# Attention and two feed-forward layers on one core: value products three units behind the scores, paired column blocks in the first layer, and an output normalised in halves

## The chip, the cores and the metric

The kernel runs on one core of a Trainium2 chip. The metric is device time in microseconds (us), the median of several runs. A profiled execution gives the trace; its engines are PE (TensorE matmul, with PEld for its weight loads), DVE (VectorE), ACT (ScalarE), POOL (GpSimd) and SP, which here issues all DMAs, transposes among them, from one queue in order. The wide matrix products use pairs of fp16 numbers, a high and a low part, so that each product of two matrices is three matmuls: high by high, high by low, low by high.

## The reference

Clustered attention with 2 batches, 8 heads, 768 positions and head size 64: queries and keys are assigned to the nearest of 16 centroids, and scores between different clusters are masked. Its output, as 1536 tokens of 512 features, goes through two feed-forward layers.

```python
q_assign = np.argmax(np.einsum('bhsd,hcd->bhsc', q_n, c_n), axis=-1)
k_assign = np.argmax(np.einsum('bhsd,hcd->bhsc', k_n, c_n), axis=-1)
mask = q_assign[:, :, :, None] == k_assign[:, :, None, :]
scores = np.where(mask, scale * np.matmul(q, k.transpose(0, 1, 3, 2)), -1000000000.0)
attn = np.exp(scores - np.max(scores, axis=-1, keepdims=True))
attn = attn / (np.sum(attn, axis=-1, keepdims=True) + 1e-09)
x = np.matmul(attn, v)                        # then (1536, 512)
...
h = x @ w_in                                  # layer 1: 512 -> 2048 -> 512
x = (h * (1.0 / (1.0 + np.exp(-h)))) @ w_out
...
h = x @ w2_in                                 # layer 2: 512 -> 2048 -> 512
out = (np.maximum(h, 0.0) + alpha * np.minimum(h, 0.0)) @ w2_out
```

## The kernel before

**Attention.** A unit is one head of one tile of 128 queries: 12 tiles by 8 heads are 96 units, u = 0 to 95. `front(u)` makes the scores (4 matmuls, L458 and L462, into one of two `s` buffers of PSUM), takes their maximum (DVE, L474), the exponential (ACT, L480), its fp16 high part (ACT, L487) and low part (DVE, L489). `front_t(u)` transposes both parts by a DMA (L495) into one of three `pt` buffers. `back(u)` makes the value product from them (18 matmuls, L507, into the one `x` tile). In the program text `back(u - LAG)` stands behind `front(u)`, with `LAG = 2`. After the eighth head of a tile `x_done` multiplies by the inverse sums (L533), makes a high and a low part (L536, L537) and transposes them (L538) as input of layer 1.

**Layer 1** (`layer1`) takes the 12 tiles in seven chunks: two of one tile, five of two. For each of 16 column blocks it makes 12 matmuls into a PSUM tile (L834), then tanh (ACT, L840), a DVE operation that also reads the PSUM tile (L841), the high part (ACT, L844) and the low part (DVE, L845). Then 16 steps of 12 matmuls make the output (L865). A step of L834 is called an A step here, A0 to A111 over the whole kernel, and a step of L865 a B step, B0 to B111.

**Weights.** They arrive as 64-bit numbers in eight pieces per matrix. A piece is loaded (SP, L561), put together as fp32 (ACT L572; ACT L576 or POOL L580; DVE L583 and L586), its squares are summed (ACT L612, and a small matmul with a matrix of ones, L211), and it is scaled and split (POOL L593, L605, L607, L609; DVE L594). The two matrices of layer 2 are loaded over the attention's keys and queries, so their loads wait for the last scores. The scale of the first layer-2 matrix is per piece; that of the second needs the sums of all its eight pieces.

**Layer 2** runs three times over 512 tokens: `split_x2` makes high and low parts of its input (DVE L924), L937 the 16 column blocks (12 matmuls each, called C), with DVE L946, L947 and L951 and ACT L950 between, and L968 the output (called D).

**What sets the order.** Program order is a hand-written interleaving: `UNITS_BY_CHUNK`, `W_TASKS` and `W2_TASKS` say how many units and weight pieces go with each step of layer 1. The framework then orders the instructions of each engine with a timeline of its own, so the order on an engine is not that of the text; it is fixed when the kernel is built, and each engine works through its own list. `issue_after(later, earlier)` adds an order between two instructions to that.

## Time and profile before

| | |
|---|---|
| runs | 878.33 us median of 3 (874.54 to 878.88) |
| profiled execution | 873.64 us; its span from first to last instruction 871.5 us |
| mean granted clock of TensorE | 0.931 of full speed |
| busy share of the span | PE 81%, PEld 56%, DVE 70%, ACT 54%, POOL 18% |
| PE idle before value products (L507), for a transpose | 78.9 us in 48 waits |

The busy shares are means over stages that differ: attention with layer-1 weights, attention with layer 1, conversion of the layer-2 weights, and layer 2. PE's bars are modelled, so a busy PE is not PE at its peak.

### The profile page before, as it was taken

What the parts mean: (1) busy time and instruction counts of PE and PEld (TensorE: products, weight loads), DVE (VectorE), ACT (ScalarE), POOL (GpSimd) and SP (SyncE); (2) the same over time, 40 slices, a digit from 0 to 9 for tenths busy, and PEclk for the clock granted to TensorE, in tenths of its full rate; (3) what the DMA queues carried; (4) which work ended last, traced back from release to release, by engine and by line L of the source; (5) the groups of instructions that cost most, each with busy time, mean ns of one, the idle gap of its engine ahead of it and who ended that gap; (6) DMA issues with size and microseconds to landing.
All of it is one profiled execution on the core that took longest, in us unless ns stands there. A gap on an engine that the chain in (4) does not pass through costs nothing.

```text
span 871.5 us, 16209 instructions
## 1 busy us (share of the span) xinstructions
PE 704.7 (81%) x6484; PEld 487.1 (56%) x6484; DVE 607.4 (70%) x1302; ACT 468.5 (54%) x861; POOL 153.5 (18%) x117
## 2 busy tenths in 40 slices
PE   2435267777887997899898869789969999999998
PEld 1323146675766776788677758667424444444443
DVE  6999988888967777875986777786993058206700
ACT  7837576647857664755765577868541023002200
POOL 5734520340201220000000004341190000000000
PEclk9995567689999999999999999999999999999999
DMA  9999878659896786784778687353100000000000
GB/s 278 235 229 249 252 177 134 122 118 163 143 173 115 119 166 98 138 140 73 123 123 139 118 222 177 116 201 139 48 1 13 24 13 1 13 25 12 1 25 25
DMA packets 241595, 101.86 MB, mean 117 GB/s; under 512 B 217328, under 2 KB 227568, under 8 KB 241392
## 3 DMA queue, kind: packets, MB, share of 16 engines
q1 hardware_dynamic: 241520, 100.83, 54.0%
q8 instruction: 51, 0.84, 0.4%
q14 instruction: 24, 0.20, 0.1%
HBM read 44.08 MB, written 3.15 MB: 54 GB/s over the span
## 4 chain that ended last, share of the span: by engine, by line
PE 36%; DMA 12%; DVE 10%; ACT 4%; issue 2%; POOL 1%; SPq 0%; POOLq 0%; DVEq 0%; ACTq 0%
PE w L968 10%; DMA arena<-arena 8%; PE w L937 6%; PE m L968 5%; PE m L937 4%; PE w L865 3%; PE w L834 3%; DMA arena<-in_moe_w_out_dram 2%; PE x L507 2%; DMA arena<-in_moe_w_in_dram 2%; DVE arena L583 1%; DVE arena L586 1%; PE s L458 1%; PE s L462 1%; DVE arena L951 1%
## 5 line engine op out<-in xcount | busy, mean ns | idle before, releaser
L834 PEld LDWEIGHTS <-arena 128*128 128x128 f16 x1344 | 126.6, 107 | 35.1 <-issue 18.8
L834 PE MATMUL w<-arena 128*128 128x256 f16 (+1 forms) x1212 | 137.5, 273 | 10.6 <-DVE arena L841 8.5
L507 PE MATMUL x<-arena 128*128 128x64 f16 x1728 | 75.0, 202 | 79.9 <-DMA arena<-arena 78.9
L865 PEld LDWEIGHTS <-arena 128*128 128x128 f16 x1344 | 118.5, 100 | 20.7 <-POOL arena L605 2.9
L865 PE MATMUL w<-arena 128*128 128x256 f16 (+1 forms) x1200 | 123.9, 260 | 5.4 <-POOL arena L605 2.5
L507 PEld LDWEIGHTS <-arena 128*128 128x128 f16 x1728 | 66.2, 104 | 95.4 <-DMA arena<-arena 91.8
L489 DVE TENSOR_TENSOR arena<-arena 128x768 f16<-128x768 f32 x96 | 95.0, 991 | 32.3 <-ACT arena L487 32.0
L474 DVE TENSOR_REDUCE stat<-s 128x1 f32<-128x768 f32 x96 | 91.1, 951 | 28.4 <-PE s L462 28.2
L480 ACT ACTIVATE arena<-s,stat 128x768 f32<-128x768 f32 x96 | 94.5, 985 | 26.3 <-DVE stat L478 25.5
L487 ACT ACTIVATE arena<-arena 128x768 f16<-128x768 f32 x96 | 80.5, 842 | 42.0 <-DMA arena<-arena 41.0
L937 PEld LDWEIGHTS <-arena 128*128 128x128 f16 x576 | 57.0, 99 | 80.0 <-issue 15.5
L968 PEld LDWEIGHTS <-arena 128*128 128x128 f16 x576 | 56.4, 98 | 68.0
L580 POOL TENSOR_SCALAR arena<-arena 128x1024 f32<-128x1024 f32 x28 | 43.2, 1541 | 287.2 <-DMA arena<-in_moe_w_in_dram 219.1
L937 PE MATMUL w<-arena 128*128 128x512 f16 x384 | 87.7, 383 | 5.3 <-DVE arena L947 5.3
L458 PE MATMUL s<-arena 80*128 80x384 f16 x192 | 69.8, 364 | 17.6 <-DMA arena<-arena 11.1
L968 PE MATMUL w<-arena 128*128 128x512 f16 x384 | 83.9, 379 | 0.0
L950 ACT ACTIVATE arena<-arena,stat 128x512 f16<-128x512 f32 x48 | 34.5, 720 | 88.2 <-DVE arena L947 86.2
L462 PE MATMUL s<-arena 128*128 128x384 f16 x192 | 69.8, 364 | 0.0
L840 ACT ACTIVATE arena<-w,stat 128x256 f32<-128x256 f32 (+1 forms) x101 | 43.5, 434 | 29.3 <-PE w L834 24.2
L583 DVE SCALAR_TENSOR_TENSOR arena<-arena 128x1024 int32<-128x1024 int32 x32 | 42.9, 1340 | 22.1 <-ACT arena L572 8.3
L946 DVE TENSOR_SCALAR arena<-w,stat 128x512 f32<-128x512 f32 x32 | 24.0, 749 | 46.9 <-PE w L937 46.5
L845 DVE SCALAR_TENSOR_TENSOR arena<-arena 128x256 f16<-128x256 f32 (+1 forms) x112 | 49.7, 451 | 6.0 <-ACT arena L844 5.9
(137 smaller groups left out, 1014.1 us busy)
## 6 DMA issues: line engine op xcount, KB each, us to landing
arena<-in_moe_w_in_dram SPq DMA_DIRECT2D x16, 1024.0 KB, 5.9
arena<-in_moe_w_out_dram SPq DMA_DIRECT2D x16, 1024.0 KB, 5.1
arena<-in_k_dram SPq DMA_DIRECT2D x8, 384.0 KB, 3.8
arena<-in_q_dram SPq DMA_DIRECT2D x6, 512.0 KB, 4.9
arena<-in_v_dram SPq DMA_DIRECT2D x8, 384.0 KB, 5.8
out_dram<-arena SPq DMA_DIRECT2D x12, 256.0 KB, 2.0
arena<-arena SPq DMA_TRANSPOSE x149, 3.9
arena<-in_moe_alpha_dram SPq DMA_DIRECT2D x1, 1024.0 KB, 4.7
```

Of the source, the lines that this page charges most:

```text
L458: nc.tensor.matmul(out=sc[:, j, :hs], lhsT=qt2[0:D + C, h], rhs=kt2[0:D + C, h % 2, j * hs:(j + 1) * hs], start=True, stop=False,)
L462: nc.tensor.matmul(out=sc[:, j, :hs], lhsT=qt1[:, h], rhs=kt1[:, h % 2, j * hs:(j + 1) * hs], start=False, stop=True,)
L474: nc.vector.tensor_reduce(out=nm, in_=sc[:, :, :hs], axis=AX.XY, op=ALU.max, negate=True)
L480: nc.scalar.activation(out=view(o, F32, 2, hs), in_=sc[:, :, :hs], func=ACTF.Exp, scale=scl, bias=bias, accum_out=sums[n % 2][:, h:h + 1],)
L487: nc.scalar.activation(out=hl[:, 0], in_=p, func=ACTF.Copy)
L489: en.tensor_tensor(out=hl[:, 1], in0=p, in1=hl[:, 0], op=ALU.subtract)
L507: nc.tensor.matmul(out=x_ps[0][:, h], lhsT=pt[:, ph * T + t], rhs=vt[:, h % 2, t, vh], start=(i == 0), stop=(i == 3 * T - 1),)
L583: nc.vector.scalar_tensor_tensor(out=lo, in0=hi, scalar=3, in1=lo, op0=ALU.logical_shift_left, op1=ALU.bitwise_or)
L834: nc.tensor.matmul(out=hp, lhsT=wi[:, a, kd, f % 2 * 128:f % 2 * 128 + 128], rhs=mov(bb, kd), start=(i == 0), stop=(i == 3 * KD - 1),)
L865: nc.tensor.matmul(out=acc, lhsT=wo[:, a, f % 2, dt * 128:(dt + 1) * 128], rhs=g[:, f, bb], start=(i == 0), stop=(i == 3 * KF - 1),)
L937: nc.tensor.matmul(out=hp, lhsT=in_piece(o_a + 24 * KB, f // 2)[:, a, kd, f % 2 * 128:][:, :128], rhs=x[bb][:, kd], start=(i == 0), stop=( ...
L968: nc.tensor.matmul(out=acc, lhsT=g[:, f, a, t * 128:(t + 1) * 128], rhs=out_piece(o_w, f // 2)[:, bb, f % 2], start=(i == 0), stop=(i == 3 ...
```

## The change

The value product of unit u is held behind the scores of unit u + 3: `LAG` is 3, and `issue_after` ties the first of its matmuls to the last score matmul of u + 3. `layer1` works on two column blocks at a time: 24 matmuls go into the two halves of one PSUM tile, and tanh, the two DVE operations and the high part each run once over both. `x_done` does its three DVE operations once for each half of the heads, over one smaller buffer `xf`. The buffer of layer 1's intermediate grows from 3 pieces of 1 KB to 2 of 2 KB, and the last targets of `UNITS_BY_CHUNK` are 99, the number of units plus the new lag. The rest of the program text is unchanged.

```diff
-UNITS_BY_CHUNK = (32, 53, 64, 69, 98, 98, 98)
+UNITS_BY_CHUNK = (32, 53, 64, 69, 99, 99, 99)
...
-            nc.tensor.matmul(
+            s_last[u] = nc.tensor.matmul(
                 out=sc[:, j, :hs], lhsT=qt1[:, h],
...
-                nc.tensor.matmul(
+                mm = nc.tensor.matmul(
                     out=x_ps[0][:, h], lhsT=pt[:, ph * T + t], rhs=vt[:, h % 2, t, vh],
                     start=(i == 0), stop=(i == 3 * T - 1),
                 )
+                if i == 0 and u + LAG in s_last:
+                    issue_after(mm, s_last[u + LAG])
...
-        nc.vector.tensor_tensor(out=xf, in0=x_ps[0], in1=bc(rs, D), op=ALU.mult)
...
+        for w in range(2):
+            xf = view(o_xf, F32, 4, D)
+            nc.vector.tensor_tensor(
+                out=xf, in0=x_ps[0][:, 4 * w:4 * w + 4], in1=bc(rs[:, 4 * w:4 * w + 4], D),
+                op=ALU.mult,
+            )
+            xf = view(o_xf, F32, DM // 2)
+            nc.vector.tensor_copy(out=xhl[:, 0, w], in_=xf)
+            nc.vector.tensor_tensor(out=xhl[:, 1, w], in0=xf, in1=xhl[:, 0, w], op=ALU.subtract)
...
-    LAG = 2
+    LAG = 3
...
-        for f in range(KF):
-            j = f // 2
+        for j in range(NPC):
...
-            hp = psum("l", n)
...
+            hp = psum("l", 2, n)
+            for r in range(2):
+                i = 0
+                for kd in range(KD):
+                    for a, bb in ((0, 0), (0, 1), (1, 0)):
+                        nc.tensor.matmul(
+                            out=hp[:, r], lhsT=wi[:, a, kd, r * 128:r * 128 + 128], rhs=mov(bb, kd),
+                            start=(i == 0), stop=(i == 3 * KD - 1),
+                        )
+                        i += 1
+                if r == 0:
+                    yield
+            th = view(o_tmp + 2 * KB * ring("t1", 2), F32, 2, n)
+            nc.scalar.activation(out=th, in_=hp, func=ACTF.Tanh, scale=dh[:, j:j + 1])
             nc.vector.scalar_tensor_tensor(
                 out=th, in0=th, scalar=1.0, in1=hp, op0=ALU.add, op1=ALU.mult
             )
...
+            hi, lo = g[:, 2 * j:2 * j + 2, 0], g[:, 2 * j:2 * j + 2, 1]
+            nc.scalar.activation(out=hi, in_=th, func=ACTF.Copy, scale=2.0 ** -16)
             nc.vector.scalar_tensor_tensor(
...
+                out=lo, in0=th, scalar=2.0 ** -16, in1=hi, op0=ALU.mult, op1=ALU.subtract,
             )
             yield
```

Since the framework orders each engine anew, instructions move far from the edited lines too. Three places matter below. The first is on PE, around the scores of the last unit, u = 95. Before, they stand between two A steps:

```order
L834 MATMUL w<-arena 128x256
L458 LDWEIGHTS arena
L458 MATMUL s<-arena 128x384
L462 LDWEIGHTS arena
L462 MATMUL s<-arena 128x384
...
L834 LDWEIGHTS arena
L834 MATMUL m<-arena 128x256
```

In the change they stand in the middle of chunk 5's B steps (L874 is the old L865, L459 and L463 the old L458 and L462):

```order
L874 MATMUL w<-arena 128x256
L459 LDWEIGHTS arena
L459 MATMUL s<-arena 128x384
L463 LDWEIGHTS arena
L463 MATMUL s<-arena 128x384
...
L874 LDWEIGHTS arena
L874 MATMUL w<-arena 128x256
```

Counted over the whole lists, 92 A steps, 80 B steps and 92 value products stand ahead of these scores before, and 96 A steps, 88 and a quarter B steps and 91 value products in the change.

The second place is also on PE, at the small sums of the second layer-2 matrix (L211 into `s`; L211 into `m` are those of `split_x2`). Before, the last seven of them stand in three places among the last B steps and the first C steps (L937); here are the second three and the last:

```order
L937 MATMUL w<-arena 128x512
L211 MATMUL s<-stat,arena 128x1 x3
L937 LDWEIGHTS arena
...
L937 MATMUL w<-arena 128x512
L211 MATMUL s<-stat,arena 128x1
L937 LDWEIGHTS arena
```

In the change all seven stand together, and the sums of `split_x2` behind them, ahead of the first C step (L946 is the old L937):

```order
L874 MATMUL w<-arena 128x256
L211 MATMUL s<-stat,arena 128x1 x7
L211 MATMUL m<-stat,arena 128x1 x4
L946 LDWEIGHTS arena
L946 MATMUL m<-arena 128x512
```

Eight C steps stood ahead of the last sum before, and none does in the change.

The third place is on DVE, from the scale of the second layer-2 matrix on (L160 from `s`). Before, DVE has the first pass of layer 2 under way there, and the two low parts that it makes for the weights (L594) stand among its rows:

```order
L160 TENSOR_SCALAR stat<-s 128x1
L951 SCALAR_TENSOR_TENSOR arena<-arena,stat 128x512
L947 SCALAR_TENSOR_TENSOR arena<-w,arena 128x512
...
L594 SCALAR_TENSOR_TENSOR arena<-arena,stat 128x1024
L946 TENSOR_SCALAR arena<-w,stat 128x512
L947 SCALAR_TENSOR_TENSOR arena<-w,arena 128x512
L594 SCALAR_TENSOR_TENSOR arena<-arena,stat 128x1024
```

In the change both low parts (L601) come first, then the split of the first pass's input (L933, the old L924), and only then its first row (L955, the old L946):

```order
L593 SCALAR_TENSOR_TENSOR arena<-arena 128x1024
L160 TENSOR_SCALAR stat<-s 128x1
...
L689 TENSOR_SCALAR stat<-stat 128x8
L601 SCALAR_TENSOR_TENSOR arena<-arena,stat 128x1024 x2
L160 TENSOR_SCALAR stat<-m 128x1
...
L933 SCALAR_TENSOR_TENSOR arena<-arena,stat 128x512 x4
L955 TENSOR_SCALAR arena<-m,stat 128x512
```

POOL's list is the same at this place in both: one piece for the first of these low parts, two multiplications of other pieces, and then the piece for the second.

## Rows read from the trace of the kernel before

**Rows 1.** Busy time by stage: start:end, PE, PEld, DVE, ACT, POOL, clock, DMA
```profile
0.00:135.00 135.00, 57.73 (x568) 43.26 (x569) 122.30 (x273) 93.77 (x154) 60.51 (x61) 0.76 0.94 235
135.00:293.00 158.00, 121.83 (x1772) 103.02 (x1770) 128.08 (x322) 105.36 (x224) 30.27 (x19) 0.90 0.80 138
293.00:509.00 216.00, 191.55 (x2246) 157.09 (x2247) 160.82 (x407) 134.55 (x263) 7.33 (x6) 0.98 0.70 122
509.00:603.00 94.00, 78.88 (x732) 67.94 (x730) 72.66 (x128) 72.78 (x135) 29.40 (x18) 0.96 0.60 180
603.00:660.00 57.00, 47.05 (x211) 21.33 (x209) 51.13 (x66) 26.88 (x39) 26.03 (x14) 0.94 0.09 32
660.00:872.00 212.00, 207.66 (x967) 94.42 (x965) 72.37 (x111) 35.12 (x50) 0.00 (x0) 1.00 0.04 15
```

**Rows 2.** Waits of PE from 135 to 293 us: us, times, longest
```profile
PE x L507 <- DMA arena<-arena: 25.7, 19, 2.6
```

**Rows 3.** Waits of PE from 293 to 509 us
```profile
PE x L507 <- DMA arena<-arena: 15.4, 16, 2.2
```

**Rows 4.** Timeline of PE, value products that waited: first and last, of 35
```profile
141.03 0.70 PE L507 MATMUL x<-arena 128*128 128x64 f16 x18 [2.14 <-DMA arena<-arena]
...
505.88 0.70 PE L507 MATMUL x<-arena 128*128 128x64 f16 x18 [1.29 <-DMA arena<-arena]
```

**Rows 5.** Chain that ended last: start us, us, what
```profile
391.80 7.86 PE w L865 x72
...
611.80 4.92 DMA arena<-in_moe_w_out_dram
...
630.13 3.13 POOL arena L607 x2
...
637.07 1.52 DVE arena L951
...
655.31 4.34 PE m L937 x12
659.65 10.36 PE w L968 x48
...
701.09 2.59 PE m L937 x12
```

**Rows 6.** Timeline of PE, 508 to 626 us: start us, us, what
```profile
508.38 0.33 PE L458 MATMUL s<-arena 80*128 80x384 f16 x1
...
559.67 2.72 PE L834 MATMUL m<-arena 128*128 128x256 f16 x12 [2.13 <-DVE arena L841]
...
602.67 5.34 PE L937 MATMUL w<-arena 128*128 128x512 f16 x24
...
625.00 0.28 PE L211 MATMUL s<-stat,arena 128*128 128x1 f32 x2
```

**Rows 7.** Groups by line, shapes apart: count, busy us, mean ns, idle before
```profile
L841 DVE SCALAR_TENSOR_TENSOR arena<-arena,w 128x256 f32<-128x256 f32 x69 | 28.5, 414 | 5.0 <-ACT arena L840 5.0
L845 DVE SCALAR_TENSOR_TENSOR arena<-arena 128x256 f16<-128x256 f32 x80 | 39.3, 495 | 5.7 <-ACT arena L844 5.7
L947 DVE SCALAR_TENSOR_TENSOR arena<-w,arena 128x512 f32<-128x512 f32 x32 | 22.0, 687 | 0.3
L583 DVE SCALAR_TENSOR_TENSOR arena<-arena 128x1024 int32<-128x1024 int32 x32 | 42.9, 1340 | 22.1 <-ACT arena L572 8.3 <-ACT arena L576 6.8 <-POOL arena L580 4.7
L533 DVE TENSOR_TENSOR arena<-x,stat 128x512 f32<-128x512 f32 x12 | 8.2, 683 | 2.6 <-PE x L507 2.6
L536 DVE CAST arena<-arena 128x512 f16<-128x512 f32 x12 | 5.0, 420 | 0.1
L537 DVE TENSOR_TENSOR arena<-arena 128x512 f16<-128x512 f32 x12 | 9.7, 806 | 0.1
```

**Rows 8.** Timeline of DVE: one kind of operation, alone and beside POOL
```profile
612.39 0.75 DVE L951 SCALAR_TENSOR_TENSOR arena<-arena,stat 128x512 f16<-128x512 f32 x1
...
643.06 2.69 DVE L951 SCALAR_TENSOR_TENSOR arena<-arena,stat 128x512 f16<-128x512 f32 x1
```

More of the change, by code (lines that the diff above doesn't have):

```diff
@@ L117, in cluster_attention_silu_prelu @@
     o_xt = region(12 * KB)
-    o_tmp = region(3 * KB)
+    o_tmp = region(4 * KB)
     o_a = region(0)
@@ L129, in cluster_attention_silu_prelu @@
     o_pt = region(NPT * 3 * KB)
-    o_xf = region(2 * KB)
+    o_xf = region(KB)
     o_xhl = region(2 * KB)
@@ L251, in prep_centroids2 @@
         sq = view(o_xf + 256, F32, D)
-        cc = view(o_xf + 512, F16, 3, 128)
+        cc = view(o_xhl, F16, 3, 128)
         ss, y, r = scr(1), scr(1), scr(1)
@@ L445, in cluster_attention_silu_prelu @@
     pt_of = {}
+    s_last = {}
     x_ps = {}
@@ L524, in x_done @@
         assert c < 3 or c - 3 in g1_done
-        xf = view(o_xf, F32, H, D)
         rs = scr(H)
@@ L532, in x_done @@
         )
-        nc.vector.tensor_tensor(out=xf, in0=x_ps[0], in1=bc(rs, D), op=ALU.mult)
-        xf = view(o_xf, F32, DM)
-        xhl = view(o_xhl, F16, 2, DM)
-        nc.vector.tensor_copy(out=xhl[:, 0], in_=xf)
-        nc.vector.tensor_tensor(out=xhl[:, 1], in0=xf, in1=xhl[:, 0], op=ALU.subtract)
+        xhl = view(o_xhl, F16, 2, 2, DM // 2)
+        for w in range(2):
[7 more added lines that the diff above has]
+            nc.vector.tensor_tensor(out=xhl[:, 1, w], in0=xf, in1=xhl[:, 0, w], op=ALU.subtract)
         nc.sync.dma_start_transpose(
             out=view(o_xt + 4 * KB * (c % 3) + 2 * KB * i, F16, 2 * KD, 128),
-            in_=xhl.rearrange("p a b -> p (a b)"),
+            in_=view(o_xhl, F16, 2 * DM),
         )
@@ L821, in layer1 @@
             nc.vector.tensor_scalar(dh, w1["in"].inv, x_inv[b], 0.5, op0=ALU.mult, op1=ALU.mult)
-        for f in range(KF):
-            j = f // 2
+        for j in range(NPC):
             wi = in_piece(o_w, j)
-            if c == 0 and f % 2 == 0:
+            if c == 0:
                 nc.vector.tensor_scalar(
@@ L829, in layer1 @@
                 )
-            hp = psum("l", n)
-            i = 0
-            for kd in range(KD):
-                for a, bb in ((0, 0), (0, 1), (1, 0)):
-                    nc.tensor.matmul(
-                        out=hp, lhsT=wi[:, a, kd, f % 2 * 128:f % 2 * 128 + 128], rhs=mov(bb, kd),
-                        start=(i == 0), stop=(i == 3 * KD - 1),
-                    )
-                    i += 1
-            th = view(o_tmp + KB * ring("t1", 3), F32, n)
-            nc.scalar.activation(out=th, in_=hp, func=ACTF.Tanh, scale=dh[:, f // 2:f // 2 + 1])
+            hp = psum("l", 2, n)
[12 more added lines that the diff above has]
+            nc.scalar.activation(out=th, in_=hp, func=ACTF.Tanh, scale=dh[:, j:j + 1])
             nc.vector.scalar_tensor_tensor(
@@ L843, in layer1 @@
             )
-            nc.scalar.activation(out=g[:, f, 0], in_=th, func=ACTF.Copy, scale=2.0 ** -16)
+            hi, lo = g[:, 2 * j:2 * j + 2, 0], g[:, 2 * j:2 * j + 2, 1]
+            nc.scalar.activation(out=hi, in_=th, func=ACTF.Copy, scale=2.0 ** -16)
             nc.vector.scalar_tensor_tensor(
-                out=g[:, f, 1], in0=th, scalar=2.0 ** -16, in1=g[:, f, 0],
-                op0=ALU.mult, op1=ALU.subtract,
+                out=lo, in0=th, scalar=2.0 ** -16, in1=hi, op0=ALU.mult, op1=ALU.subtract,
             )
```

## The prediction, made before the kernel ran

> **What bounds the kernel now.** I read the busy time by stage first [rows 1]. Up to 135 us DVE is busy for 122.3 of 135 us: layer-1 weights and the first 16 units load it, and nothing that only helps PE pays there. From 135 to 509 us PE has 313 us of work in 374, DVE 289: neither is full, but PE is nearer. From 509 to 603 us PE, DVE and ACT are each at 77 to 84%; this stage converts the layer-2 weights while PE finishes layer 1. From 603 to 660 us DVE is busy 51 of 57 us. From 660 us on PE does layer 2 almost without a gap, 212 us that the change does not touch.
>
> Next the waits of PE. Before value products it waited for transposes for 25.7 us and 15.4 us in the two middle stages [rows 2, 3], 41.1 us of the 61 us that PE was idle there. Such waits before 135 us lie under DVE.
>
> Last, the chain that ended last [rows 5]. Its tail is no attention: a load of the second layer-2 matrix at 611.80, POOL's multiplications at 630.13, DVE at 637.07, then the last C step at 655.31 and the first D step at 659.65. The loads it goes through must wait for the last scores, at 508.38 [rows 6], since they overwrite keys. So the end is a sum of four parts: last scores at 508.4; from there to the last small sum of the second matrix 116.6 (to 625.00 [rows 6]); from that sum to the first D step 34.6; and 214.0 from there to the end of the profiled 873.64 us.
>
> **The change, part by part.**
>
> *Work put ahead of the last scores.* By the lists, 12.25 more steps of 12 matmuls stand ahead of them, and one value product less. The chain has 72 matmuls in 7.86 us [rows 5], so a step is 1.31 us: +16.0, less 0.7 for the value product [rows 4], **+15.3 us**. This work is not new, it is only earlier; what it is worth depends on whether its old place was on the path, and after 509 us it was not.
>
> *Waits before value products.* The lag of 2 in the text is not the lag on the engine. Counted in PE's list before, 47 of the 79 value products between 135 and 509 us already stand exactly three units behind, 13 stand four behind and 19 closer. Counted from the timeline, of which [rows 4] has the first and last waiting row of 35, the 47 waited 0.53 us each and the 13 waited 0.72: a larger lag alone bought nothing. What does move is the work between a unit's last score and its value product: summed with the step above, units 16 to 91 have 12.0 us of it on average before and 14.7 in the change, because more layer-1 steps stand between. The five value products with 16 us or more between waited 0.12 us each, those with 10 to 12 us 0.57. Bounds: nothing gained (the order only moves the wait), or all 41.1. I take six tenths, **-24 us**, since 14.7 lies between those two groups, nearer to the second in work and to the first in what a further step brings.
>
> *Two column blocks at once.* Per pair two DVE operations, not four. L841 at twice the width should cost like L947, which also reads PSUM at 512 columns: 0.687 against 2 x 0.414; L845 like L951 undisturbed, 0.75 [rows 8], against 2 x 0.495 [rows 7]. That is 0.38 us per pair, and I use it for the 16 narrow pairs too, as the saving is fixed cost: 56 x 0.38 = 21 us of DVE, ACT saving about as much. Halving the output normalisation adds three operations per tile: between nothing and 1.91 us (the sum of L533, L536, L537, if a half cost as much as the whole); I take the fixed cost of the pairs, 0.14 to 0.24 each, 0.5 us per tile, +6 us over 12 tiles. Net 15 us less DVE work over the kernel, but only the stage before 135 us and the stages after 509 us are near DVE's limit: **-4 us** up to the last scores. A pair's elementwise work starts one step later, 1.31 us; the B steps that follow read it last, after 14 of 16 blocks, which covers it.
>
> So the last scores come at 508.4 + 15.3 - 24 - 4 = **495.7 us**.
>
> *From there to the last small sum.* Before, 20 A steps' DVE work (20 x 0.91 = 18 us) and that of eight C steps (8 x 2.1 = 17 us: L947 at 0.69, L951 at 0.75, and L946 taken like L947) competed with the weights in these 116.6 us; now it is eight pairs (8 x 1.44 = 12 us) and no C step. Bounds: 116.6, if the loads and the chain per piece (load 4.9 us, [rows 5]) set the pace alone; 94, if all of these 23 us come off. I take **98**: towards the end DVE's list has seven pieces in a row with nothing between.
>
> *From the sum to the first D step.* Here the new order costs. Before, eight C steps were done when the last sum came, and the rest took 34.6 us. Now the first C step waits for all sums, and on DVE for both low parts, of which the second needs POOL to have gone through two other multiplications; that low part ended at 637.07 before, 12.1 us after the sum. With the input's split behind it, about 2.5 us (some of it beside POOL, where L951 took 2.69 instead of 0.75 [rows 8]), C begins 14.5 us after the sum. Then 16 C steps of 2.59 us [rows 5], 41.4 us, and the last block's elementwise work, about 1.8. That is 57.7. PE will have been idle between its last B step and this: about 54 us of work remains after the last scores, against 98 + 14.5. In the trace a wait of 2.13 us was followed by 12 matmuls at 2.72 us, twice the 1.31 of a step, which is what the lower of the two clock levels (1.2 GHz, not 2.4) would give [rows 6]; the granted clock of the stage is 0.94 [rows 1]. So I add one C step at half speed, 2.6: **60 us**, between 49 (POOL's wait overlapped) and 66.
>
> The Trainium skill ("TensorE: Matmul & The Clock Gate", section "What's actually happening") calls the throttled state the default, which activity releases. The trace agrees with the doubled step after a wait; by that rule every gap that the change opens would be paid twice, and the sum with a second slow C step would be 2.6 us longer.
>
> *Sum.* 495.7 + 98 + 60 = 653.7 for the first D step, against 659.65: 5.9 us less, 867.7 us against the profiled 873.64. The median of the runs is 4.7 us above the profiled execution; by the same offset the forecast is **872 us**.
>
> **The rivals.**
>
> *The waits go almost entirely.* With 3 us more work between, only early units wait. Last scores at 508.4 + 15.3 - 41 - 4 = 479, first D step at 637: 851 us profiled, 855 by the median. For it: the five products that had the most work between. Against: waits at 14 to 16 us of work, ten products, were still 0.6 us each.
>
> *The layer-2 start swallows more than is won* (the slower side). Waits fall by only 10 us and the weights, bound by loads and the chain of each piece, keep 110 of their 116.6 us: last scores at 510, first D step at 680, 894 profiled, 898 by the median. It decides against the change as soon as these two stages together take longer than the 151.2 us of before (116.6 + 34.6) by more than the last scores come earlier. For it: L583, the first DVE step of a piece, waited 22 us, most of it for ACT [rows 7], so DVE is not all that paces the pieces, and no C step is hidden any more. Half of this loss gives 888.
>
> *The lag is no change at all.* The lists had it already; waits stay at 41 us, the 15.3 us of early work were in slack, and the two later stages cancel. That is 877 to 880.
>
> **How the numbers follow.** I tell no change from 0.5%, 4.4 us, about the spread of the runs shown: faster means below 873.9, slower above 882.7. The forecast (865 to 879) has 0.40, the waits gone (850 to 865) 0.25, the swallowed gain (over 882) 0.25, the lag no change 0.10. Of the forecast's 0.40 some 0.25 lies below 873.9. Faster 0.25 + 0.25 = 0.50; slower 0.25; same 0.25. The range leaves out a tenth on each side: from 850, all waits gone, to 892, most of the swallowed gain.
>
> **What would show it.** Last scores (L459) starting near 496 us; waits of PE for transposes before value products near 17 us after 135 us; L850 near 0.69 us and L855 near 0.75 at full width; the seven sums near 594 us, the first C step near 608 with PE idle before it, the first D step near 654, and 212 us behind it as before. I am wrong if the waits before value products do not depend on the work between, if the pieces of weights come no faster with DVE free, or if the first C step does not wait for the second low part.

## The result and the profile after

The changed kernel takes **881.85 us** (median of 15 runs, 878.16 to 884.39), the kernel before 875.45 us beside it (873.15 to 879.71): ratio **1.0064**, 95% interval 1.0046 to 1.0082. It is slower by 0.6%; 872 us, so faster, had been forecast.

The four parts of the forecast's sum, from the profiled executions (spans 871.5 and 880.1 us):

| part, us | before | forecast | changed |
|---|---|---|---|
| last scores | 508.4 | 495.7 | 502.1 |
| from there to the last small sum | 116.6 | 98 | 106.8 |
| from that sum to the first D step | 34.6 | 60 | 56.6 |
| first D step | 659.5 | 653.7 | 665.5 |

Busy time by stage in the changed kernel (start:end, length, PE, PEld, DVE, ACT, POOL, then granted clock, DMA share, GB/s), to be read against [rows 1]:

```profile
0.00:135.00 135.00, 55.01 (x556) 39.83 (x557) 122.71 (x267) 91.85 (x147) 53.95 (x61) 0.97 0.96 240
135.00:293.00 158.00, 133.06 (x1899) 114.07 (x1897) 124.83 (x299) 102.44 (x190) 31.14 (x19) 0.92 0.76 133
293.00:509.00 216.00, 196.23 (x2334) 163.67 (x2331) 164.90 (x395) 132.10 (x227) 6.92 (x5) 0.94 0.74 130
509.00:603.00 94.00, 59.18 (x530) 50.77 (x527) 65.68 (x89) 58.36 (x80) 32.13 (x19) 0.85 0.57 179
603.00:660.00 57.00, 40.19 (x173) 19.04 (x174) 44.30 (x59) 30.86 (x54) 23.92 (x13) 0.77 0.00 2
```

From 135 to 509 us PE does 16 us more work in the same time: the gain up to the last scores. From 509 to 660 us it does 26.6 us less than before, and every other engine but POOL is less busy too. That every engine has time to spare points to an order of the work rather than to a busy engine. The waits of PE from 509 to 662 us (total, times, longest) name it:

```profile
PE s L211 <- ACT arena L619: 31.2, 5, 9.2
PE m L211 <- ACT arena L923: 7.7, 1, 7.7
PE w L841 <- DVE arena L850: 4.5, 2, 2.8
```

The timeline of PE, the answer to [rows 6], shows where they lie:

```profile
573.77 10.64 PE L874 MATMUL w<-arena 128*128 128x256 f16 x96
588.16 1.44 PE L211 MATMUL s<-stat,arena 128*128 128x1 f32 x6 [3.75 <-ACT arena L619]
598.84 1.44 PE L211 MATMUL s<-stat,arena 128*128 128x1 f32 x6 [9.24 <-ACT arena L619]
608.89 0.59 PE L211 MATMUL s<-stat,arena 128*128 128x1 f32 x2 [8.61 <-ACT arena L619]
617.18 1.86 PE L211 MATMUL m<-stat,arena 128*128 128x1 f32 x8 [7.70 <-ACT arena L923]
621.24 0.59 PE L946 MATMUL m<-arena 128*128 128x512 f16 x1 [2.20 <-ACT arena L932]
```

PE is through with layer 1 at 584.4 us, 18.4 us earlier than before (602.8). Before, the first C step follows at once. Now 37 us pass, 31.5 of them in waits: for the squares of seven weight pieces (ACT L619, 21.6 us), then for those of `split_x2` (ACT L923) and for its high part (ACT L932). On ACT the squares of `split_x2` begin only behind the last small sum:

```profile
608.66 0.18 ACT L619 ACTIVATION_READ_ACCUMULATOR arena<-arena 128x1 f32 x1
609.52 0.63 ACT L923 ACTIVATE arena<-arena 128x512 bf16<-128x512 f32 x1 [0.68 <-PE s L211]
```

The releaser of that row is the clue to all that follows: a square of layer 2's input, which is ready well before (in e9 below, the sums of these squares run at 578.5 us), waits for a *small sum of a weight matrix*, on which it depends by no number. The scratch to which `split_x2` writes its squares is `junk = view(o_a + 84 * KB, ...)`, at a fixed offset. The regions from `o_a` to the matrix of ones (`o_one`), which `all_sum` multiplies by, add up to 85 KB before and to 84 KB in the change, since `o_xf` shrank from 2 KB to 1. So the scratch, until then on idle parts of the normalisation, now lies on the matrix of ones. The framework keeps writes behind the reads of the same place, and thus these squares behind every small sum ahead of them in the text. (The splits' own sums are then made with overwritten ones, so their scale can be another power of two than before; the work is the same.)

The edits themselves, by groups with shapes apart (count, busy us, mean ns, idle before), answer to [rows 7]:

```profile
L850 DVE SCALAR_TENSOR_TENSOR arena<-arena,w 128x512 f32<-128x512 f32 x34 | 23.2, 681 | 0.9 <-ACT arena L849 0.7
L855 DVE SCALAR_TENSOR_TENSOR arena<-arena 128x512 f16<-128x512 f32 x40 | 28.5, 716 | 3.5 <-ACT arena L854 3.5
L538 DVE TENSOR_TENSOR arena<-x,stat 128x256 f32<-128x256 f32 x24 | 10.1, 420 | 6.3 <-PE x L508 4.8 <-PE m L431 1.4
L543 DVE CAST arena<-arena 128x256 f16<-128x256 f32 x24 | 8.9, 369 | 0.2
L544 DVE TENSOR_TENSOR arena<-arena 128x256 f16<-128x256 f32 x24 | 12.1, 503 | 0.2
```

A pair costs 0.681 us where two single operations cost 2 x 0.414, and 0.716 against 2 x 0.495: 0.42 us less per wide pair, 0.38 forecast. A tile's normalisation costs 2 x (0.420 + 0.369 + 0.503) = 2.58 us instead of 1.91: 0.68 more, 0.5 forecast. As means of single operations these terms were near. DVE as a whole gained less: all its durations together fell by 12.7 us, for 15 forecast, and its busy time, in which neighbours overlap, only by 5.8 (607.35 to 601.51 us).

### The profile page after: what moved, and what is told of

It reads as the page before. It is cut to its first block, busy times and chain, and to the rows that moved or that the text cites. A ratio compares the mean times of both kernels' runs of the same rounds, so it can differ in the third digit from the quotient of the medians.

```text
span 880.1 us, 16024 instructions
## 1 busy us (share of the span) xinstructions
PE 699.9 (80%) x6484; PEld 485.7 (55%) x6484; DVE 601.5 (68%) x1226; ACT 453.0 (51%) x749; POOL 148.1 (17%) x117
## 4 chain that ended last, share of the span: by engine, by line
PE 34%; issue 25%; DMA 16%; DVE 15%; ACT 6%; POOL 3%; SPq 1%; POOLq 0%; DVEq 0%; ACTq 0%
PE w L977 9%; PE w L946 9%; DMA arena<-arena 8%; PE m L977 5%; PE m L946 4%; DMA arena<-in_moe_w_out_dram 4%; DVE arena L601 2%; DVE arena L593 2%; PE w L874 2%; DVE arena L590 2%; PE w L841 2%; DMA arena<-in_moe_w_in_dram 2%; DVE arena L490 2%; DVE stat L475 1%; PE x L508 1%
## 5 line engine op out<-in xcount | busy, mean ns | idle before, releaser
L841 PEld LDWEIGHTS <-arena 128*128 128x128 f16 x1344 | 120.5, 102 | 29.8 <-issue 9.5
L841 PE MATMUL w<-arena 128*128 128x256 f16 (+1 forms) x1200 | 127.9, 263 | 9.7 <-DMA arena<-arena 5.2
L874 PE MATMUL w<-arena 128*128 128x256 f16 (+1 forms) x1248 | 128.9, 262 | 7.9 <-POOL arena L612 3.5
L874 PEld LDWEIGHTS <-arena 128*128 128x128 f16 x1344 | 119.7, 101 | 22.7 <-POOL arena L612 3.8
L490 DVE TENSOR_TENSOR arena<-arena 128x768 f16<-128x768 f32 x96 | 96.8, 1010 | 27.6 <-ACT arena L488 27.4
L508 PE MATMUL x<-arena 128*128 128x64 f16 x1728 | 72.6, 201 | 53.0 <-DMA arena<-arena 45.2
L508 PEld LDWEIGHTS <-arena 128*128 128x128 f16 x1728 | 66.0, 103 | 66.1 <-DMA arena<-arena 53.0
L946 PEld LDWEIGHTS <-arena 128*128 128x128 f16 x576 | 57.2, 99 | 73.5 <-issue 8.2
L977 PEld LDWEIGHTS <-arena 128*128 128x128 f16 x576 | 56.4, 98 | 67.9
L459 PE MATMUL s<-arena 80*128 80x384 f16 x192 | 70.0, 365 | 25.9 <-ACT arena L481 17.0
L946 PE MATMUL w<-arena 128*128 128x512 f16 x384 | 88.5, 385 | 0.0
L587 POOL TENSOR_SCALAR arena<-arena 128x1024 f32<-128x1024 f32 x28 | 37.8, 1348 | 283.5 <-issue 192.2
L955 DVE TENSOR_SCALAR arena<-w,stat 128x512 f32<-128x512 f32 x32 | 23.9, 749 | 89.0 <-PE w L946 88.6
L977 PE MATMUL w<-arena 128*128 128x512 f16 x384 | 84.0, 379 | 0.0
L463 PE MATMUL s<-arena 128*128 128x384 f16 x192 | 70.5, 367 | 0.0
L619 ACT ACTIVATE arena<-arena 128x1024 f32<-128x1024 f32 x32 | 36.6, 1142 | 38.4 <-DVE arena L593 38.4
L579 ACT ACTIVATE arena<-arena 128x1024 int32<-128x1024 uint32 x32 | 36.3, 1136 | 29.0 <-DMA arena<-in_moe_w_out_dram 17.4
```

The source lines that it names most:

```text
L459: nc.tensor.matmul(out=sc[:, j, :hs], lhsT=qt2[0:D + C, h], rhs=kt2[0:D + C, h % 2, j * hs:(j + 1) * hs], start=True, stop=False,)
L463: s_last[u] = nc.tensor.matmul(out=sc[:, j, :hs], lhsT=qt1[:, h], rhs=kt1[:, h % 2, j * hs:(j + 1) * hs], start=False, stop=True,)
L490: en.tensor_tensor(out=hl[:, 1], in0=p, in1=hl[:, 0], op=ALU.subtract)
L508: mm = nc.tensor.matmul(out=x_ps[0][:, h], lhsT=pt[:, ph * T + t], rhs=vt[:, h % 2, t, vh], start=(i == 0), stop=(i == 3 * T - 1),)
L841: nc.tensor.matmul(out=hp[:, r], lhsT=wi[:, a, kd, r * 128:r * 128 + 128], rhs=mov(bb, kd), start=(i == 0), stop=(i == 3 * KD - 1),)
L874: nc.tensor.matmul(out=acc, lhsT=wo[:, a, f % 2, dt * 128:(dt + 1) * 128], rhs=g[:, f, bb], start=(i == 0), stop=(i == 3 * KF - 1),)
```

## The experiments

Each kernel's main points, from its profiled execution, with the ratio of its runs to the kernel before on the same chip (95% interval):

| kernel | last scores | last sum | first C | first D | ratio |
|---|---|---|---|---|---|
| before | 508.4 | 625.0 | 602.7 | 659.5 | 1 |
| changed | 502.1 | 608.9 | 621.2 | 665.5 | 1.0064 (1.0046 to 1.0082) |
| e1_lag | 510.4 | 625.4 | 599.3 | 662.9 | 1.0003 (0.9974 to 1.0032) |
| e2_pair_half | 513.5 | 627.4 | 639.7 | 684.0 | 1.0261 (1.0228 to 1.0295) |
| e3_half | 526.5 | 634.2 | 652.5 | 696.6 | 1.0397 (1.0367 to 1.0427) |
| e4_tail | 499.3 | 613.3 | 587.2 | 645.5 | 0.9826 (0.9798 to 0.9853) |
| e5_scratch_after | 503.6 | 612.8 | 603.7 | 656.4 | 0.9952 (0.9929 to 0.9974) |
| e6_scratch_before | 511.7 | 617.5 | 636.1 | 680.0 | 1.0200 (1.0165 to 1.0235) |
| e7_whole | 514.4 | 625.2 | 631.6 | 675.8 | 1.0204 (1.0171 to 1.0236) |
| e8_tail_clean | 499.1 | 627.1 | 605.8 | 662.4 | 1.0034 (1.0009 to 1.0059) |
| e9_scratch_free | 501.9 | 617.2 | 587.3 | 645.6 | 0.9813 (0.9781 to 0.9844) |
| e10_half_free | 524.4 | 636.7 | 614.7 | 673.1 | 1.0157 (1.0113 to 1.0201) |
| e11_pair_half_free | 515.1 | 636.7 | 597.9 | 652.1 | 0.9870 (0.9831 to 0.9909) |
| e12_before_moved | 505.7 | 619.5 | 603.1 | 655.0 | 0.9972 (0.9945 to 0.9998) |
| e13_no_tie | 507.2 | 628.7 | 587.9 | 642.4 | 0.9794 (0.9761 to 0.9826) |
| e14_sums_late | 498.9 | 614.2 | 582.5 | 640.8 | 0.9793 (0.9762 to 0.9824) |

In the changed kernel, e2 and e7 the last C step of the first pass stands behind the first 17 matmuls of D. Their first D step so has 15 C steps ahead of it, and 16 in all others; counted alike it is 2.6 us later.

### The parts of the change alone, and another tail

The first theory was that the framework's own timeline had put the seven sums ahead of the first C step; the overlap was not yet seen.

**e1_lag**, the lag alone on the kernel before:

```diff
-    LAG = 2
+    LAG = 3
...
+                if i == 0 and u + LAG in s_last:
+                    issue_after(mm, s_last[u + LAG])
```

> The kernel before with the lag alone: LAG 3, the tie of the value product to the scores of u + 3, unit targets 99; single column blocks and whole output normalisation as before. On PE the last sums of the second layer-2 matrix then stand among the first eight C steps, as before, not ahead of them. Theory (the changed order behind the last sums is what costs): the last scores come near 502 us as in the changed kernel, the end then takes what it took before (116.6 + 34.6 + 214), so about 867 us profiled, ratio near 0.99. Rival (the lag itself delays attention): last scores no earlier than 508, 876 us or more, ratio 1.00 or above.

Neither: the end is as before, as the theory had it, but the last scores come no earlier (510.4). PE's waits for transposes before value products fell from 41.1 to 32.2 us (135 to 509 us), but 6.25 more layer-1 steps, 8.2 us of work, now stand ahead of these scores. Alone, the lag changes the time by nothing that shows.

**e2_pair_half**, the changed kernel without the lag:

```diff
-    LAG = 3
+    LAG = 2
...
-                if i == 0 and u + LAG in s_last:
-                    issue_after(mm, s_last[u + LAG])
```

> The changed kernel without the lag: LAG 2, no tie, unit targets 98; paired column blocks and the normalisation in halves stay. On PE all sums of the second layer-2 matrix stand ahead of the first C step, as in the changed kernel. Theory (that order is what costs): from the last scores to the first D step 160 us or more, against 151 before; with the waits before value products as before, the last scores come at 508 or later, so about 885 us, ratio 1.01 or more. Rival (the lag is what costs): the first D step comes no later than before, 659 us, ratio 0.995 or below, since about 15 us of DVE work are gone.

As the theory said, and more: 170 us from the last scores to the first D step, the whole 2.6% slower. The loss does not come with the lag.

**e3_half**, the halves alone on the kernel before:

```diff
-    o_xf = region(2 * KB)
+    o_xf = region(KB)
...
+        for w in range(2):
+            xf = view(o_xf, F32, 4, D)
```

> The kernel before with the output normalisation in halves alone (and the smaller buffer). On PE the last sums now stand between B107 and B108, with the sums of the input's split, so four B steps and all 16 C steps stand behind them. Theory (what stands behind the last sum on PE sets the end): from the last sum to the first D step 4 x 1.31 + 16 x 2.59 + 2 = 49 us, against 34.6 before; the last sum itself no more than 8 us earlier; total 880 us or more, ratio above 1.005. Rival (the halves cost 0.7 us of DVE per tile and nothing else): ratio 1.00.

4.0% slower, for 0.68 us of DVE per tile. The last scores come 18 us later (taken up with e10), and from the last sum to the first D step it is 62.5 us. So what stretches the tail comes with the halves, and besides their work they change the buffers.

**e4_tail**, the changed kernel with the split directly behind the last A step and the sums in the text behind the eighth C step:

```diff
-            if c == len(chunks) - 1 and i == KF + 4:
+            if c == len(chunks) - 1 and i == KF - 1:
                 split_x2(0)
...
+            if j == 0 and f == 7:
+                run_bg(len(bg))
+                w2["out"].scale()
+                bg.extend(w2["out"].late)
```

> The changed kernel with another order of its tail: the scale of the second layer-2 matrix, and so its sums, stands in the text behind the eighth C step, and the split of the first pass's input directly behind the last A step. All that stands ahead of the last A step on PE is as in the changed kernel. Theory (the sums ahead of the first C step cost the overlap): the first C step follows the last B step near 585 us instead of 621; C steps of 2.59 us run while the last pieces arrive; the first D step near 640 instead of 665, total near 855 us, ratio near 0.975. Rival (DVE and POOL bound this stretch, so that C steps put in front only make the pieces later): the last sum moves from 609 to 620 or later, the first D step to 655 to 660, total 870 to 876 us, ratio 0.995 to 1.00.

The theory's numbers nearly: first C step at 587.2, first D step at 645.5, 1.7% faster than before. C steps do hide the conversion when no sum stands ahead of them. (Here the seven sums are made with the overwritten ones, so the second matrix gets another scale and the kernel computes something else; e14 has nearly this tail without that.)

### The scratch

**e5_scratch_after**, one number in the changed kernel:

```diff
-        junk = view(o_a + 84 * KB, BF16, N2)
+        junk = view(o_a + 83 * KB, BF16, N2)
```

> The changed kernel with one number changed: the scratch of the squares in the split of the second layer's input lies 1 KB lower, at o_a + 83 KB, so that it is on the normalisation's high and low parts, as in the kernel before, and no longer on the matrix of ones, which moved there because the normalisation's buffer shrank. Nothing ahead of the last sums changes its place on PE. Theory (the overlap orders the squares behind every small sum that reads the ones, and that is why the first C step waits for the last sum): six sums stay ahead of the first C step and the last one goes behind C2; the first C step comes near 605 us instead of 621, the first D step near 655 instead of 665, about 870 us, ratio near 0.994. Rival (the framework's timeline puts the sums there whatever the buffers): no change, ratio 1.006.

The theory: first C step at 603.7, first D step at 656.4, ratio 1.1 points below the changed kernel. But the place overlaps something else: 80 to 84 KB also holds the seventh piece of the second matrix, so the squares now waited for that piece's sum (and wrote over the piece, whose part of the output is changed).

**e6_scratch_before**, only the overlap, put into the kernel before:

```diff
-        junk = view(o_a + 84 * KB, BF16, N2)
+        junk = view(o_a + 85 * KB, BF16, N2)
```

> The kernel before with that scratch 1 KB higher, on its matrix of ones, as the change has it: only this overlap of the change is put in. On PE the last sums then stand between B107 and B108, ahead of the input's split. Theory (the overlap alone costs what the tail of the change costs): last scores at 508 as before, last sum near 622, then four B steps and 16 C steps, first D step near 676 instead of 659, about 889 us, ratio near 1.018. Rival (it is the later value products, the pairs or the halves as work): ratio 1.00.

2.0% slower, 892.5 us where 889 was expected. PE's timeline has the same picture as the changed kernel, with four B steps caught behind the sums as well (first C step, L937, at 636.06):

```profile
617.52 0.58 PE L211 MATMUL s<-stat,arena 128*128 128x1 f32 x2 [6.12 <-ACT arena L612]
625.81 1.86 PE L211 MATMUL m<-stat,arena 128*128 128x1 f32 x8 [7.70 <-ACT arena L914]
627.92 8.31 PE L865 MATMUL m<-arena 128*128 128x256 f16 x48 [0.25 <-DVE stat L160]
636.06 2.32 PE L937 MATMUL w<-arena 128*128 128x512 f16 x10
```

**e9_scratch_free**, the changed kernel with the scratch on layer 1's intermediate buffer:

```diff
-        junk = view(o_a + 84 * KB, BF16, N2)
+        junk = view(o_tmp, BF16, N2)
```

> The changed kernel with the scratch of the squares in layer 1's intermediate buffer (o_tmp), which nothing else uses by then; in the earlier attempt at o_a + 83 KB it lay on the seventh piece of the second layer-2 matrix, and so behind that piece's sum, and spoilt that piece. Everything ahead of B104 keeps its place on PE; the first C step now stands directly behind the last B step, the last seven sums at C1, C5 and C8. Theory (the overlap with the matrix of ones is the whole cost of the tail): first C step near 586 us, first D step near 645, about 860 us, ratio near 0.983. Rival (DVE and POOL hold the C steps back once they meet the conversion): first D step 655 or later, ratio 0.995 or more.

859.7 us, 860 expected; ratio 0.9813. The last B step and the first C steps are now neighbours, and the sums stand among the C steps:

```profile
582.76 3.22 PE L874 MATMUL w<-arena 128*128 128x256 f16 x28
587.27 0.38 PE L946 MATMUL m<-arena 128*128 128x512 f16 x1 [1.29 <-ACT arena L932]
...
593.07 0.72 PE L211 MATMUL s<-stat,arena 128*128 128x1 f32 x6
...
608.05 0.73 PE L211 MATMUL s<-stat,arena 128*128 128x1 f32 x6
...
617.22 0.36 PE L211 MATMUL s<-stat,arena 128*128 128x1 f32 x2
```

Its waits of PE from 509 to 662 us, against 31.2 and 7.7 above (there is none for L923):

```profile
PE s L211 <- ACT arena L619: 11.4, 3, 6.7
PE w L946 <- DVE arena L956: 4.5, 2, 2.3
```

**e12_before_moved**, the same line in the kernel before, as a control:

```diff
-        junk = view(o_a + 84 * KB, BF16, N2)
+        junk = view(o_tmp, BF16, N2)
```

> The kernel before with its scratch in layer 1's intermediate buffer: a control. In the kernel before the scratch lies on the normalisation's parts, idle by then, so either place is free. Theory: no change, ratio 0.995 to 1.005. Rival (the new place itself is better): ratio below 0.99, and the gain of the changed kernel with the free scratch would be that of the place.

No change that could carry e9 (0.9972). So one line separates the changed kernel at 1.0064 from 0.9813, and the same overlap alone costs the old kernel 2.0%. Two more pairs below differ in that line alone: e3 and e10 (1.0397 and 1.0157), e2 and e11 (1.0261 and 0.9870).

**e8_tail_clean** and **e14_sums_late** tie the seven sums behind the eighth C step, with the split moved as in e4; e8 has the scratch at 83 KB, e14 in `o_tmp`:

```diff
-            tot = all_sum([ss[:, j:j + 1] for j in range(NPC)], kind)
+            tot = all_sum([ss[:, j:j + 1] for j in range(NPC)], kind, after)
...
+                w2["out"].scale(mm)
```

> The changed kernel with the scratch at o_a + 83 KB, the split of the first pass's input directly behind the last A step, and the sums of the second layer-2 matrix tied behind the eighth C step. Theory (C steps hide the conversion once no sum stands ahead of them): first C step near 586 us, first D step near 645, about 860 us, ratio near 0.982, as the kernel with the moved tail had it (whose own overlap made it read overwritten ones). Rival (that kernel was fast because its sums read something else): ratio above 0.99.

Neither: 1.0034. Its scratch lies on the seventh piece, as in e5, so the split's squares come behind that piece's. PE waits 15.8 us for them, its sums of the split run from 593.9 to 598.3 us, and they hold up the last B steps: the first C step comes at 605.8.

> The changed kernel with the free scratch, the input's split directly behind the last A step, and the last seven sums tied behind the eighth C step. On PE one C step more than with the free scratch alone stands ahead of the second three sums, two more ahead of the first. Theory (C steps now run as far ahead of the conversion as DVE lets them): first C step near 586, first D step within 3 us of 645, ratio 0.978 to 0.985. Rival (sums that stall PE between C steps still cost, 5 us of waits): first D step near 640, ratio 0.975.

First C step 582.5, first D step 640.8, ratio 0.9793: the ratio is in the theory's range, the first D step nearer to the rival's. The interval overlaps that of e9, so whether the sums' places still cost something is not decided.

### What the parts are worth without the overlap

**e10_half_free** is e3_half with the scratch in `o_tmp`, **e11_pair_half_free** e2_pair_half with it; the edit is that of e9.

> The kernel before with the halves alone, and the scratch in layer 1's intermediate buffer, so without the overlap. Theory (the halves have a cost of their own ahead of the last scores, and the overlap cost the rest): last scores near 526 us as with the overlap, from there to the first D step about 150 as before instead of 170, so about 891 us, ratio near 1.02. Rival (all that the halves cost came from the overlap): ratio 1.00 to 1.005.

The theory: 1.0157, last scores at 524.4. The halves alone cost the old kernel something ahead of the last scores too. Of these 16 us, 8.4 are work that moved: 6.4 more layer-1 steps stand ahead of the scores. The waits of PE from 135 to 509 us show a kind that hardly existed before (2.4 us for that line in all):

```profile
PE x L507 <- DMA arena<-arena: 33.5, 28, 2.5
PE w L838 <- DVE arena L845: 15.3, 11, 4.9
```

A steps wait for DVE to empty their PSUM tile, while DVE waits for scores (37.3 us in all and once for 8.0, against 25.7 and 4.5 in the kernel before, 135 to 530 us). The order on all engines differs from the kernel before; whether the smaller operations or that new order is to blame was not separated.

> The changed kernel without the lag and without the overlap (pairs and halves, scratch in layer 1's intermediate buffer). Theory (the lag is worth what the last scores came earlier by, 11 us): last scores near 513 us, first D step near 660, about 876 us, ratio near 1.00, against 0.983 with the lag. Rival (the lag is worth nothing, as it was when made alone, 1.0003): the same time as the kernel with the lag and the free scratch.

The last scores come at 515, as the theory said, but the time is 865 us (ratio 0.9870), not 876: only 137 us pass from there to the first D step. With the lag (e9) it is 0.9813; the two intervals overlap. Of the 13 us by which the last scores come earlier with the lag, about 5 arrive at the end.

**e13_no_tie**, e9 without the tie, with `LAG = 3` in the text:

```diff
-                if i == 0 and u + LAG in s_last:
-                    issue_after(mm, s_last[u + LAG])
```

> The changed kernel with the free scratch and LAG 3 in the text, but without the tie of the value product to the scores of u + 3. Theory (the lag in the text leaves the framework its own order, only the tie holds the value products back): the time of the kernel without any lag, 865 us, ratio 0.987, waits of PE for transposes before value products near 38 us from 135 to 509 us. Rival (the lag in the text does it): 860 us, ratio 0.981, such waits near 24 us.

The rival: 0.9794, waits before value products 25.7 us, as with the tie (23.7). The text's lag is enough. Against e11 that is 0.8 points, the intervals apart. And the last scores come at 507.2, 5 us later than in e9, with no loss in the end.

**e7_whole**, the changed kernel with the output normalised whole, its buffer shared with layer 1's intermediate:

```diff
+        xf = view(o_tmp + 2 * KB * ring("t1", 2), F32, H, D)
+        nc.vector.tensor_tensor(out=xf, in0=x_ps[0], in1=bc(rs, D), op=ALU.mult)
```

> The changed kernel with the output normalised whole again (its 2 KB buffer shares the two buffers of layer 1's intermediate, so the other regions stay) and the scratch at o_a + 83 KB. On PE 13.8 fewer steps of 12 matmuls and one value product more stand ahead of the last scores than in the changed kernel, 17.4 us less work. Theory (halves only add 0.7 us of DVE work per tile): last scores near 502 - 17 = 485 us. Rival (the halves also hold up PE, by about 11 us, as the kernel with the halves alone suggests: last scores 18 us later with 7 us more work ahead): last scores near 474 us. With the scratch moved the C steps follow the last B step in either case; total 850 to 862 us, ratio 0.97 to 0.985.

Both missed: last scores at 514.4. Once, at 396 us, DVE waited 12.4 us for the high part of an exponential, which stood on ACT's list behind three outputs of layer 1 (L877) that had to wait for PE's B steps. Whether the shared buffer brought that order about is not shown, and the scratch again lay on the seventh piece. It tells nothing of the halves. Pairs without halves were not run otherwise.

## Why the prediction was wrong

**What failed.** Two terms of the sum were mis-sized: the conversion ("From there to the last small sum") took 106.8 us, not 98, and the waits before value products were worth 13.5 us, not 24. Together, 19.3 us, they are more than the miss of 14.4 that the profiled execution shows (below). The price of the third part was near, but it had another cause than the prediction thought.

**The step that failed in kind** is the start of layer 2 ("Here the new order costs"). The prediction saw that all sums and the split stand ahead of the first C step, and its price for it was near (60 us forecast, 56.6 measured, 59.2 with the same C steps counted). But it took that order as the framework's choice, and read the change's buffers as without effect ("Halving the output normalisation adds three operations per tile"). The order came from the smaller buffer: a false dependence through the scratch, shown by e6 (in: 2.0% slower) and e9 (out: 2.5 points faster). It also named the wrong work between sum and C: the second low part ended at 617.9, 9.0 us after the sum and not 12.1, and what came last were the split's squares on ACT, four of them between 609.5 and 617.1, which held the split's sum to 617.18 and its scale to 619. The first C step came 12.4 us after the last sum, for 14.5.

**Waits before value products, -24 us.** They fell from 41.1 us [rows 2, 3] to 21.9:

```profile
PE x L508 <- DMA arena<-arena: 13.1, 14, 2.4
...
PE s L459 <- ACT arena L481: 2.3, 3, 1.0
```

```profile
PE x L508 <- DMA arena<-arena: 8.8, 8, 2.0
PE s L459 <- ACT arena L481: 5.8, 2, 5.6
```

(135 to 293 us, then 293 to 509 us.) That is -19.2, and a new wait took some of it back: scores wait for the exponential to empty their PSUM buffer, 8.1 us against 2.4. Unit 16's scores came 2.9 us earlier (for -4), the other waits of PE fell from 16.5 to 14.3. With the 15.3 us of work ahead this makes -3.3 where -6.3 was measured; the rest, 3.0, is within what single executions differ by (below). The term was mis-sized: -13.5 where -24 stood. More work between did go with fewer waits in the changed kernel: its 35 value products with 14 us or more between waited 0.11 us each, the other 45 0.40. But work is not all that sets them: e11 and e13 have the same work between on average, within 0.2 us, and waited 37.7 and 25.7 us. What else does stays open.

**The conversion, 98 us.** It took 106.8. Four pairs of kernels differ in the overlap alone, and so in whether C steps run during the conversion: 106.8 us without them and 115.4 with them (changed, e9), 105.8 and 116.6 (e6, before), 113.8 and 121.6 (e2, e11), 107.7 and 112.4 (e3, e10). So the C steps lengthen it by 5 to 11 us, where the prediction had 17 for their DVE work alone; of the 18.6 us that it took off for C and A steps together, 9.8 came. The chain that ended last shows what else sets the pace near the end (start, us, what): loads and the steps of a piece alternate, each load waiting for the squares of an earlier piece to free its buffer.

```profile
588.13 4.88 DMA arena<-in_moe_w_out_dram
593.19 1.85 POOL arena L587
595.07 1.24 DVE arena L590
596.33 1.24 DVE arena L593
597.59 1.21 ACT arena L619 x2
598.85 4.96 DMA arena<-in_moe_w_out_dram
```

10.7 us from one load to the next, of which DVE has 2.5. That is the rival "The layer-2 start swallows more than is won", with less than half its price: 881.85 us, where half was 888.

**The sum** missed by 11.8 us at the first D step: 6.4 at the last scores, 8.8 in the conversion, 3.4 back in the tail. Most of these 3.4 are a matter of counting. The prediction put 16 C steps ahead of the first D step; the list has 15, and the last of them behind 17 matmuls of D (L977):

```profile
665.49 3.83 PE L977 MATMUL w<-arena 128*128 128x512 f16 x17
669.16 2.75 PE L946 MATMUL m<-arena 128*128 128x512 f16 x12
```

With that step the tail took 59.2 us, 60 forecast, and the miss is 14.4 us, like that of the whole profiled execution (881.85 against 867.7). In the medians the miss is only 9.9 us (881.85 against 872), and that is luck: the prediction added the 4.7 us by which the median of three runs lay above the profiled execution of the kernel before, and over 15 runs it lies 1.8 above (875.45 against 873.64). The sum of parts had a flaw of its own: the parts are not independent. e11 reached the last scores 13 us later than e9 and the first D step 6.5 us later. Without the overlap the change gives 859.7 us (0.9813), a larger gain than the forecast's.

**The clock.** From 603 to 660 us the granted clock was 0.77 in the changed kernel, 0.91 in e9, where PE idles less. After a wait of 4.18 us the next steps ran at half speed:

```profile
531.48 0.58 PE L211 MATMUL s<-stat,arena 128*128 128x1 f32 x2 [4.18 <-ACT arena L619]
531.92 5.17 PE L841 MATMUL m<-arena 128*128 128x256 f16 x24
...
551.47 2.67 PE L841 MATMUL w<-arena 128*128 128x256 f16 x23 [2.84 <-DVE arena L850]
```

2.58 us for 12 matmuls, twice 1.31, which is the lower of the two levels (granted clock 0.52 from 532 to 537 us, 1.00 from 537 to 545). The Trainium skill ("TensorE: Matmul & The Clock Gate", section "What's actually happening") says that activity releases a throttle which is otherwise there; the trace agrees. Slow clock after this wait cost PE 2.5 us, and these steps do not lie on the chain that ended last. Nor was every gap paid for twice, as the prediction had it: after the wait of 2.84 us in the last row, 23 matmuls took 2.67 us, full speed. The slow first C step that the prediction added cannot be read off, since these steps waited for the split's low parts on DVE as well.

**The pairs.** The Trainium skill ("Perfetto Trace Analysis", section "Optimizing Scalar/DVE Operations") says that every DVE operation carries a fixed access cost, so larger operations help a saturated engine. The trace agrees on the cost: by the means of these tables 0.15 us saved per L850 pair, 0.27 per L855 pair. Over 40 wide and 16 narrow pairs that is some 23 us of DVE durations. But the means of L845 and L855 hold a few long operations of 1.0 to 1.7 us (next section but one). By the medians, 0.419 us for L845 and 0.685 for a wide L855, that pair saves 0.15 too, and the three operations of the normalisation cost 0.15 to 0.16 more each for being halved, 0.47 per tile. And neighbours overlap: the split's operations on DVE (L933) alone last 0.747 us and start 0.67 us apart, so that a saved duration is more than saved time.

Pairs and halves together, without overlap and lag, are 1.3% faster than before (e11), halves alone 1.6% slower (e10). So the pairs, added to the halves, carry a gain; pairs alone were not run.

## What to carry to other kernels

When a buffer in a hand-made arena changes size, list every view at a fixed offset behind it: a scratch that slides onto a live constant may do no visible harm and still order two unrelated chains of work. When an instruction's releaser in the trace is one on whose numbers it does not depend, look for the address they share before blaming the scheduler, and test by moving the buffer alone. The new place needs the same list: 83 KB was a second overlap, and the kernels with it stayed 1.4 (e5) and 2.4 points (e8) slower than their like at a free place (e9, e14).

## What the runs showed of the hardware that was not expected

The changed kernel, e4, e5, e8, e9 and e14 have the same instructions in the same order on PE up to the last scores, yet reached these at 502.1, 499.3, 503.6, 499.1, 501.9 and 498.9 us: a single profiled execution cannot tell terms under 5 us there.

The split's low parts on DVE beside POOL took 9.97 us for four operations, where 2.5 us had been allowed for all; such an operation alone takes 0.75 [rows 8]. In the chain that ended last they are one piece; below it the same four operations in e9, during which POOL has nothing to do (timeline of DVE):

```profile
621.23 9.97 DVE arena L933 x4
...
587.52 2.73 DVE L933 SCALAR_TENSOR_TENSOR arena<-arena,stat 128x512 f16<-128x512 f32 x4
```

The first C step needs them from its second matmul on, so it begins at 621.24 us but its elementwise work only at 631.87, and the first three C steps took 12.4 us instead of 7.8. The layer-1 and normalisation operations show the same: of L845 and L537 before, and of L855, L543 and L544 in the change, 15 took longer than 0.9 us, where the medians lie between 0.28 and 0.69. POOL was at work for two thirds or more of each of the 15.
